# A gated mix of two long convolutions on one core: earlier stores of finished columns, two buffers of P rows, work moved to VectorE, a new order

## The chip, the core and the metric

The kernel runs on one core of a Trainium2 chip. The metric is device time in microseconds (us), the median of several runs. Engines are called as in the profile: PE (TensorE, matrix products; its weight loads are PEld), DVE (VectorE), ACT (ScalarE), POOL (GpSimd) and SP (SyncE, which here only issues DMAs). SP, ACT and POOL each issue DMAs from a queue of their own; all DMAs run on the same 16 DMA engines.

## What is computed

The input x is [2048, 448] (time, channel). A gate weighs two branches:

```python
g = sigmoid((x * gate_w).sum(-1, keepdims=True))
# branch A, per channel d: 256 complex modes
dt = exp(log_dt);  P = exp(dt * A * l)          # l = 0..2047
K  = einsum("dn,dnl,dn->dl", C, P, dt * B).real
a  = causal_conv(x, K) + x * Dskip              # by FFT of length 4096
# branch B
kv = shift_conv4(k) * v
b  = x * (causal_conv(kv, ssm_k) + kv * ssm_D)
out = g * a + (1 - g) * b
```

All arrays are bfloat16; the convolutions are 2048 long and causal, one per channel and branch.

## The kernel before

The convolutions are done by transforms written as matrix products, for 28 channels of each of four groups at a time, that is for 112 columns of work. H = 0 to 3 counts these column groups (`NQG = 4`, `NC = 28`). A convolution of branch B or A for one H goes through `spread_in` (products ps_c, copied by ACT into a tile zs), `transform` (ps_2 or ps, copied back to zs), a product with the transformed kernel on DVE (`products`), `stage_a` (ps_a, copied into a tile U) and `stage_b` (ps_b), whose result goes to an epilogue. The product also needs a copy of one operand with its two partition halves exchanged, zsS; `swapped` makes it with two DMAs on SP. zs, zsS, zsK and U share one pool of `NBQ = 7` buffers (tag q); a new tile waits until the last reader of the buffer is done.

The kernel K of branch A is made in eight blocks j (two for each H, class `KGen`). `Tables.levels` and `reals` fill a table ET of powers: phases on DVE (ks_ph), then sine and exponential on ACT, then a product on DVE. Of each pair cos, sin a negated copy of the first is kept as a third row (lines 652 to 661): for the Q levels by `nc.scalar.mul` on ACT, for the P levels on DVE. From ET, DVE doubles up two sets of rows: TQ, 32 rows for both blocks of an H (`q_rows`), and TP, 32 rows for each block (`block`, line 458). TP's rows 0 to 7 come from three doublings (`mult`, then `add`). Rows 8 to 15 are a sum of two products: one goes into a tile kg_P4 (kg_P in the profile), one into TP itself, and a DMA from POOL with `accum_op=ALU.add` adds the first to the second (lines 478 to 483). Rows 16 to 31 are the mirrored rows 0 to 15 times a real factor (`back`). `back(8, 16)` reads rows 0 to 7, `back(0, 8)` reads rows 8 to 15 and so waits for that DMA. 224 small products of TQ and TP follow into pk, whose copy kg_S goes through `gather` (ps_g, kg_KT) and `spread` (ps_c) into the tile zsK. The tile kg_TP has a single buffer: the rows of a block may be written only when the products of the block before have read theirs.

The last convolution, A of H = 3, is cut into halves (`transform_half`, `stage_a_half`, `last`), with block 7 between. `mix` weighs the two branches for each H on DVE in the tile ug, which is vt: for H below 3 a weighing of each and a sum, for H = 3 only the part of branch B, as branch A arrives last. Then `stage_b` with one bank runs `epilogue_A(3)` four times, each time for 16 of the 64 time steps that a partition holds: a product with the gate (ept), a sum into vt, and `store`, four DMAs of 32 partitions x 16 x 112 columns, two on SP and two on ACT.

At the start, ssm_D is added to a column of the loaded ssm_k by POOL (`sk_cols`). Constants lie in a tile scratch, which has the buffer that TP takes over later.

No engine's order comes from the program text. All calls are recorded (`Order`) and issued in the order of the string `ORDER`, which lists them by number; each engine works its own part strictly in that order. All recorded instructions therefore carry one line in the profile, L148, and are told apart by their tiles. DMAs of SP and ACT take one of eight completion semaphores each; a DMA whose semaphore was used by an earlier one waits for that one first.

## Time and profile before

| | us |
|---|---|
| three runs | 277.46, 279.8, 280.59 (median 279.8) |
| the profiled execution | 277.69 |
| its span, first to last instruction | 275.8 |
| DVE, ACT, PE busy | 241.7, 226.7, 210.7 |
| last product of block 7 into pk, end | 246.2 |
| last matmul, end | 264.1 |
| last DVE instruction, end | 266.2 |

A matmul's row gives its time in the pipeline, so PE's sums of durations are larger than its busy time. DVE and ACT instructions that follow each other overlap a little in the record. A row such as `L148 DVE TENSOR_TENSOR kg_TP<-kg_P 128x896 bf16<-128x896 bf16 x8 | 5.0, 625 | 0.1` says: eight such instructions, 5.0 us busy together, 625 ns each on average, and 0.1 us in which DVE stood idle before them. In lists of waits the three numbers are the time in all, how often, and the longest. The engine SPq in such a list is SP's queue of DMAs.

### The profile page before, as it was taken

How to read it: one execution, taken by the hardware profiler on the slowest of the kernel's cores; microseconds unless marked ns; L12 is line 12 of the kernel's file. 1: busy time of each engine (PE TensorE's matmuls, PEld its weight loads, DVE VectorE, ACT ScalarE, POOL GpSimd, SP SyncE). 2: the span in 40 equal slices, each digit the busy share in tenths (PEclk: the TensorE clock that was granted, in tenths of full speed). 3: DMA queues.
4: the chain of work that ended last, by engine and by line, in shares of the span. 5: the costliest groups of instructions: out<-in, count | busy, mean ns of one | idle time of the engine just before them, and what ended most of it. 6: DMA issues, size and time to landing. Idle time of an engine off the chain costs nothing.

```text
span 275.8 us, 12739 instructions
## 1 busy us (share of the span) xinstructions
PE 210.7 (76%) x5770; PEld 193.3 (70%) x5770; DVE 241.7 (88%) x488; ACT 226.7 (82%) x383; POOL 15.9 (6%) x51
## 2 busy tenths in 40 slices
PE   0610958879988799798997789867887999699830
PEld 0500858877887798687995779766886899688820
DVE  7599899999989799979996899899999997967950
ACT  2795696999899999998998799999999989546400
POOL 8000000000400000100010001001001001000000
PEclk9999999999999899998998999999999999979975
DMA  7999799607804500390093019003042263600077
GB/s 149 224 204 172 131 235 175 99 1 153 118 5 91 116 5 4 83 186 5 5 209 47 5 50 199 10 2 70 6 90 64 54 138 60 147 5 2 2 141 127
DMA packets 55110, 24.74 MB, mean 90 GB/s; under 512 B 49680, under 2 KB 52368, under 8 KB 55056
## 3 DMA queue, kind: packets, MB, share of 16 engines
q1 hardware_dynamic: 48640, 19.34, 37.7%
q0 software_dynamic: 1152, 3.67, 7.2%
q10 hardware_dynamic: 5264, 0.92, 2.1%
q8 instruction: 45, 0.74, 1.2%
q14 instruction: 9, 0.07, 0.1%
HBM read 7.95 MB, written 2.87 MB: 39 GB/s over the span
## 4 chain that ended last, share of the span: by engine, by line
ACT 38%; PE 29%; DVE 15%; DMA 9%; issue 5%; SPq 0%; DVEq 0%; POOL 0%; POOLq 0%; ACTq 0%
ACT zs L148 15%; ACT ET L148 7%; ACT U L148 6%; DMA kg_TP<-kg_P 6%; PE pk L148 5%; PE ps_a L148 5%; PE ps L148 5%; PE ps_c L148 5%; PE ps_b L148 5%; ACT zsK L148 5%; DVE vt L148 2%; DVE scratch L148 2%; PE ps_g L148 2%; PE ps_gate L148 2%; DMA skraw<-in_B_ssm_k_dram 2%
## 5 line engine op out<-in xcount | busy, mean ns | idle before, releaser
L148 ACT CAST zs<-ps 128x896 bf16<-128x896 f32 x48 | 44.0, 944 | 1.0 <-PE ps L148 0.6
L148 ACT CAST zs<-ps_c 128x1024 bf16<-128x1024 f32 (+1 forms) x48 | 42.7, 937 | 1.3 <-PE ps_c L148 1.2
L148 PEld LDWEIGHTS <-front 128*32 128x32 bf16 (+1 forms) x496 | 19.1, 159 | 27.3 <-issue 22.3
L148 PEld LDWEIGHTS <-s_W 128*128 128x128 bf16 x544 | 28.9, 100 | 12.7 <-issue 9.6
L148 PE MATMUL pk<-kg_TP,kg_TQ 128*32 128x32 bf16 x1792 | 33.2, 242 | 5.1 <-issue 2.9
L148 PEld LDWEIGHTS <-kg_TQ 128*32 128x32 bf16 x1792 | 31.2, 160 | 7.0 <-issue 4.8
L148 PE MATMUL ps_a<-sa_R,zs 128*128 128x128 bf16 x224 | 32.7, 235 | 0.3
L148 ACT CAST U<-ps_a 128x1024 bf16<-128x1024 f32 (+1 forms) x30 | 27.2, 936 | 6.9 <-PE ps_a L148 6.7
L148 PE MATMUL ps_b<-U,sb_G 128*128 128x28 bf16 x1024 | 29.5, 175 | 4.1 <-issue 1.4
L148 PE MATMUL ps_a<-sa_R,zsS 128*128 128x128 bf16 x224 | 32.1, 232 | 0.5 <-DVE zsS L148 0.5
L148 PE MATMUL ps<-zs,s_W 128*128 128x112 bf16 x384 | 27.7, 220 | 5.5 <-ACT zs L148 4.2
L148 PEld LDWEIGHTS <-sb_G 128*128 128x128 bf16 x1024 | 27.8, 96 | 5.8 <-issue 3.2
L148 DVE TENSOR_TENSOR kg_TP<-kg_TP,ET 128x1792 bf16<-128x1792 bf16 x24 | 26.1, 1090 | 5.8 <-DMA kg_TP<-kg_P 5.0
L148 PEld LDWEIGHTS <-zsS 128*128 128x128 bf16 x224 | 29.6, 152 | 1.3 <-DVE zsS L148 0.7
L148 PEld LDWEIGHTS <-zs 128*128 128x128 bf16 x224 | 29.4, 151 | 0.8
L148 PE MATMUL ps_v<-front 128*32 128x336 bf16 (+3 forms) x448 | 16.0, 310 | 16.0 <-DVE front L148 13.1
L148 ACT ACTIVATE ET<-ks_ph 128x448 bf16<-128x448 int16 x40 | 23.2, 602 | 4.1 <-DVE kg_P L148 2.6
L148 DVE TENSOR_TENSOR kg_TQ<-kg_TQ,ET 128x896 bf16<-128x896 bf16 (+1 forms) x36 | 24.8, 730 | 0.0
L148 DVE TENSOR_TENSOR kg_P<-kg_TP,ET 128x1792 bf16<-128x1792 bf16 (+1 forms) x24 | 22.4, 934 | 0.1
L148 PE MATMUL ps_c<-Wc,uu 128*64 128x128 bf16 x224 | 18.4, 290 | 1.6 <-ACT U L148 0.6
L148 PE MATMUL ps_c<-Wc,vt 128*64 128x128 bf16 x224 | 17.1, 285 | 1.4 <-ACT zs L148 1.2
L148 PEld LDWEIGHTS <-uu 128*64 128x64 bf16 x224 | 16.5, 210 | 2.4 <-issue 1.5
(102 smaller groups left out, 427.4 us busy)
## 6 DMA issues: line engine op xcount, KB each, us to landing
zsS<-zs SPq DMA_DIRECT2D x16, 448.0 KB, 5.7
kg_TP<-kg_P POOLq DMA_DIRECT2D x8, 448.0 KB, 5.7
vt<-in_B_v_dram SPq DMA_DIRECT2D x4, 448.0 KB, 6.8
skraw<-in_B_ssm_k_dram SPq DMA_DIRECT2D x16, 112.0 KB, 4.8
uu<-in_A_u_dram SPq DMA_DIRECT2D x4, 448.0 KB, 8.5
ks_xf<-xfd SPq DMA_DIRECT2D x3, 336.0 KB, 3.3
out_dram<-vt ACTq DMA_DIRECT2D x8, 112.0 KB, 3.8
out_dram<-vt SPq DMA_DIRECT2D x8, 112.0 KB, 3.6
```

What stands on the lines that cost most here:

```text
L148: ins = f(*args, **kw)
```

## The change

Six edits, and a new order for all calls:

- `mix` stores columns 0 to 83 of each group (H below 3) with four DMAs on SP, after the sums; `store` then writes only columns 84 to 111 in each of its 16 DMAs. A row of the first kind has 168 bytes, one of the second 56, where it had 224.
- TP lies in one tile of 48 rows, taken once. Rows 0 to 15 of it serve even blocks, 16 to 31 odd ones, 32 to 47 hold the mirrored rows of every block. The matmul's access pattern steps from the first kind to the second by `far`. `NBQ` goes from 7 to 6; scratch, which has the same buffer, grows with it.
- In block 7, rows 8 to 15 are made by two `mult` and two `add` on DVE; in the others the sum by DMA stays, in a function `summed`.
- The negations of the Q levels run on DVE.
- The addition of ssm_D runs on DVE.
- `ORDER` is replaced as a whole.

```diff
-NBQ = 7
+NBQ = 6
...
+    def summed(self, dst, src, r, m):
+        n = src.shape[1]
+        part = self.pool.tile([P, 8 * 2 * M], bf16, name="kg_P4", tag="kg_P4", bufs=2)[:, 0:n * 2 * m]
+        for c, out in enumerate((part.rearrange("p (n v m) -> p n v m", n=n, v=2), dst)):
+            self.nc.vector.tensor_tensor(out=out, in0=src[:, :, c].unsqueeze(2).to_broadcast([P, n, 2, m]),
+                                         in1=bass.AP(r.tensor, r.offset + c * m, [list(r.ap[0]), [0, n], [-m, 2], [1, m]]), op=ALU.mult)
+        self.nc.gpsimd.dma_start(dst.rearrange("p n v m -> p (n v m)"), part, accum_op=ALU.add)
...
-        TP = self.pool.tile([P, 32, 2, M], bf16, name="kg_TP")
+        if j == 0:
+            self.TA = self.pool.tile([P, 48, 2, M], bf16, name="kg_TP")
+        TP, late = self.TA[:, 16 * (j % 2):16 * (j % 2) + 16], self.TA[:, 32:48]
+        far = 16 * (2 - j % 2)
...
-            V.tensor_tensor(out=TP[:, 16 + i0:16 + i1], in0=src,
+            V.tensor_tensor(out=late[:, i0:i1], in0=src,
...
-        part = self.pool.tile([P, 8, 2 * M], bf16, name="kg_P4", tag="kg_P4", bufs=2)
-        r = EP[:, entry_of(64) - EQ_N + 1]
-        for c, out in enumerate((part.rearrange("p n (v m) -> p n v m", v=2), TP[:, 8:16])):
-            V.tensor_tensor(out=out, in0=TP[:, 0:8, c].unsqueeze(2).to_broadcast([P, 8, 2, M]),
-                            in1=bass.AP(r.tensor, r.offset + c * M, [list(r.ap[0]), [0, 8], [-M, 2], [1, M]]), op=ALU.mult)
-        nc.gpsimd.dma_start(TP[:, 8:16].rearrange("p n c m -> p (n c m)"), part.rearrange("p n x -> p (n x)"), accum_op=ALU.add)
+        if j == NBLK - 1:
+            add(8, mult(TP[:, 0:4], 64))
+            add(12, mult(TP[:, 4:8], 64))
+        else:
+            self.summed(TP[:, 8:16], TP[:, 0:8], EP[:, entry_of(64) - EQ_N + 1], M)
...
-                        rhs = bass.AP(r0.tensor, r0.offset, [list(r0.ap[0]), [32 * M + (1 - 2 * c) * M, 2], [2 * M, 16]])
+                        rhs = bass.AP(r0.tensor, r0.offset, [list(r0.ap[0]), [2 * M * far + (1 - 2 * c) * M, 2], [2 * M, 16]])
...
-                    nc.scalar.mul(B[:, :, 2], B[:, :, 0], -1.0)
+                    V.tensor_scalar(out=B[:, :, 2], in0=B[:, :, 0], scalar1=-1.0, scalar2=None, op0=ALU.mult)
...
-        nc.gpsimd.tensor_tensor(out=raw[:, :, 0], in0=raw[:, :, 0], in1=dB[:, H * NC:(H + 1) * NC], op=ALU.add)
+        V.tensor_tensor(out=raw[:, :, 0], in0=raw[:, :, 0], in1=dB[:, H * NC:(H + 1) * NC], op=ALU.add)
...
-    cons = Consts(nc, wp, kgp.tile([P, 3584], i32, name="scratch", tag="kg_TP"))
+    cons = Consts(nc, wp, kgp.tile([P, 5376], i32, name="scratch", tag="kg_TP"))
...
-    def store(b0, n):
+    def store(b0, n, c0, c1):
         for g in range(4):
-            dmae[g % 2].dma_start(out4[g][:, b0:b0 + n, :], ug[g * 32:(g + 1) * 32, b0:b0 + n, :])
+            dmae[g % 2].dma_start(out4[g][:, b0:b0 + n, c0:c1], ug[g * 32:(g + 1) * 32, b0:b0 + n, c0:c1])
...
-            store(b0, n)
+            store(b0, n, (NQG - 1) * NC, 112)
...
+        done = (NQG - 1) * NC
+        for g in range(4):
+            nc.sync.dma_start(out4[g][:, :, 0:done], ug[g * 32:(g + 1) * 32, :, 0:done])
```

## The prediction

> **What bounds the kernel now.** I read the whole span first: the page's engine table, then four stretches of it, cut at the first ScalarE copy of a transform (48 us), at the end of the seventh block's pk product (225), at the last matmul (264.2) and at the last packets (274).

> ```profile
> PE 210.7 (76%) x5770; PEld 193.3 (70%) x5770; DVE 241.7 (88%) x488; ACT 226.7 (82%) x383; POOL 15.9 (6%) x51
> ```
> ```profile
> 0.00:48.00 48.00, 22.13 (x520) 19.94 (x521) 42.16 (x141) 33.32 (x63) 6.67 (x41) 1.00 1.08 184
> 48.00:225.00 177.00, 153.46 (x4208) 140.44 (x4207) 166.09 (x305) 169.35 (x289) 8.33 (x9) 0.97 0.36 70
> 225.00:264.20 39.20, 35.14 (x1053) 32.93 (x1046) 31.63 (x40) 24.01 (x33) 0.85 (x1) 0.96 0.20 42
> 264.20:274.00 9.80, 0.00 (x0) 0.00 (x0) 1.86 (x4) 0.00 (x0) 0.00 (x0) 0.54 1.03 181
> ```
> Columns after the length: PE, weight loads, DVE, ACT, POOL, clock, DMA share, GB/s. So there are four limits. At the start DVE has 5.8 us free of 48 and ACT 14.7. In the middle ACT has 7.7 free of 177 and DVE 10.9: both carry it. From 225 to the last matmul PE has 4.1 free of 39.2. After that it is DMA alone: share 1.03, 181 GB/s, PE and ACT done; DVE ends at 266.2, the packets at about 273.5.

> Next, what DVE waited for in all, and its order of time around the last block.

> ```profile
> DVE kg_TP L148 <- DMA kg_TP<-kg_P: 5.0, 3, 2.1
> ...
> DVE kg_KT L148 <- PE ps_g L148: 3.4, 1, 3.4
> ...
> DVE kg_TP L148 <- PE pk L148: 1.4, 2, 0.8
> ```
> ```profile
> 225.20 0.28 DVE L148 TENSOR_TENSOR kg_TP<-kg_P 128x224 bf16<-128x224 bf16 x1 [0.56 <-PE pk L148]
> ...
> 230.52 1.08 DVE L148 TENSOR_TENSOR kg_TP<-kg_TP,ET 128x1792 bf16<-128x1792 bf16 x1
> ...
> 235.69 1.09 DVE L148 TENSOR_TENSOR kg_TP<-kg_TP,ET 128x1792 bf16<-128x1792 bf16 x1
> ```
> The P rows of block 7 start only when the product of block 6 has read theirs (225.2); their last step starts at 235.69, after the accumulating DMA, so 11.6 us pass from free buffer to finished rows.

> The rows that price the edits, by shape (busy, mean ns, idle before), and three waits of SP:

> ```profile
> L148 ACT ACT_TABLE_LOAD x11 | 14.1, 1283 | 2.9 <-issue 2.8
> ...
> L148 ACT ACTIVATE ET<-ET 128x448 bf16<-128x448 bf16 x8 | 5.1, 638 | 1.0 <-DVE ET L148 1.0
> ...
> L148 DVE TENSOR_TENSOR kg_TP<-kg_P 128x896 bf16<-128x896 bf16 x8 | 5.0, 625 | 0.1
> ...
> L148 DVE TENSOR_SCALAR ET<-ET 128x448 bf16<-128x448 bf16 x8 | 2.2, 274 | 0.0
> ...
> L148 ACT ACTIVATE ET<-ET 128x224 bf16<-128x224 bf16 x4 | 1.8, 440 | 0.0
> ```
> ```profile
> SPq L148 <- PE ps_a L148: 20.5, 4, 8.0
> ...
> SPq L148 <- DMA out_dram<-vt: 2.7, 3, 1.9
> SPq L1040 <- DMA out_dram<-vt: 2.5, 2, 2.1
> ```

> The execution profiled took 277.69 us, its span 275.8, so 1.9 lie outside. The three runs are 277.46, 279.8 and 280.59: the median is 2.1 above the profiled one. I sum against 277.7 and add 2.1 at the end.

> **Q negations.** Twelve leave ACT: 8 x 638 + 4 x 440 = 6.9 us, three of them in the start, so 6 x 638 + 3 x 440 = 5.1 in the middle. DVE takes them at its own negation row, 274 ns, less the 0.09 by which DVE instructions overlap in order of time (229.52 + 1.08 ends after the next start, 230.52): 12 x 0.19 = 2.2, of which 1.7 in the middle.

> **D added on DVE.** Four additions of 128x28 leave POOL. No DVE row has that shape; the nearest are 145 ns (one column) and 268 ns (128x224): 0.6 to 1.1 us in all, I take 0.7, nearer the small shape. On POOL they stood only before the accumulating DMAs; nobody else waited there.

> **P rows in two buffers.** The first 16 rows alternate, the mirrored 16 stay single and still wait for the product before. In DVE's new order the work between the second multiplication and the step that needs the DMA is 7 to 22 us in six blocks (before: 5 to 10); the DMA lands 4.3 to 8.2 us after its issue, 0.85 more on POOL. One block (6) keeps 4.7. So of the 5.0 us that DVE waited for this DMA I take 4 off, between 2 and 5, and the 1.4 for pk goes. The cover is DVE's own work; if that comes late, up to 1.5 us a block return.

> **Last block summed on DVE.** Two multiplications stay two multiplications; two additions of 896 come in: 2 x (0.625 - 0.09) = 1.1 us on DVE, and POOL's 0.85 plus the landing go. Only the two mirrored steps and the additions stand behind the product of block 6: 1.0 + 1.1 + 1.0 = 3.1 us where 11.6 passed.

> **Middle, 48 to 225.** ACT loses 5.1 of work. DVE gains 1.7 + 0.4 and loses 4 + 0.6 of waiting: 2.5 less. Were each free of the other, the stretch would be 2.5 to 5 us shorter; waits between engines move rather than vanish, so I take 2.0, with bounds +2.1 (only the added DVE work shows) and -5.1. The rest of the new order moves work and adds none. On SP up to four loads of skraw now stand ahead of the first swap, 4 x 0.62 = 2.5 us of issue; that swap went out at 63.0 and lands 5.7 later, and DVE's product first reads it at 79.6, so 11 us hide it.

> **End, 225 to the last DVE step.** The 8.5 us that the P chain loses can give no more than PE's 4.1 us of slack, since nearly all its 35.1 us remain behind block 6. Late next is PE itself; DVE's share (31.6 + 1.1 + mixing) is just below. I take -3.0, bounds 0 and -4.1.

> **Start.** The built order has 16 table loads for 11, and all five extra ones stand before ACT's first copy of a transform: 5 x 1.283 = 6.4 us, less three negations (1.7): 4.7 more on ACT. It had 14.7 us free there, while DVE, the bound, has 0.7 more work before the last product into vt. I take 0, bounds -1 and +4.7.
> [...]

> **Stores.** Before, 16 DMAs of 512 packets of 224 bytes: 8,192 packets keep the 16 DMA engines busy from 263 to 273.5. Now the 16 move 56 bytes a packet, and four more of 2,048 packets of 168 bytes go out first, on SP. The trace's packet records give 13.0 ns for 8 bytes (mean), 15.7 for 128, 19.0 for 224 on ACT's queue. Between them I put 56 bytes at 14.1 and 168 at 17.1: 8,192 x 14.1 / 16 = 7.2 us and 8.8 us, against 10.5 us of DMA share summed over the tail before. The early four are released by the third addition of the mixing; 9.8 us of DVE work stand behind it in the new order. They need about 3 us to issue and land near DVE's end; DMAs were idle there (share 0.02 from 240 to 260). SP's third and fourth late stores take their completion semaphores over from early ones, and so wait for them, with the rest of SP's queue behind. So the late stores end between 0.4 + 3.2 = 3.6 us after DVE's end (last issue and shortest landing) and 7.3 (as before). I take 5.3: -2.0.

> Sum: -2.0 - 3.0 + 0 - 2.0 = -7.0; 277.7 - 7.0 = 270.7; with 2.1, 272.8. I say 273.

> **Rivals.**
> A packet costs the same at 56 bytes as at 224. For it: 8-byte packets take 13.0 ns, not a twenty-eighth of 19.0. Against: 128 bytes have 15.7. Then the late stores again need 10.5 us and the tail is as long as before: 275. [...] Chance 0.10.
> The waits only move: DVE keeps the 24.5 us in which it stood until 266.2 (266.2 - 241.7), and its 2.2 + 0.7 + 1.1 = 4.0 us come on top, with the tail's -2.0: 281.8. For it: three engines carry the middle. Against: the waits for the accumulating DMA are named. Chance 0.13.
> The start: all 4.7 us of added ACT work show, since ACT ends the start (its first copy waits at 48): 277.5. Against: 14.7 us free. Chance 0.09.
> Slower: six large working buffers for seven. Before, SP's swap DMAs already waited 20.5 us in four waits for a stage A (ps_a) to give a buffer free. With one buffer less each swap after the first may go out one stage later: 56 matmuls, 63 ns from start to start, 3.5 us; seven convolutions, 24.5 us. Against: no compute engine is named as waiting for a swap, so it has slack, 40.7 us of SP's waits being for DVE instead. It outweighs the gain of 7 once 0.29 of it shows; at a half it is 273 + 12.3 = 285. Chance 0.18.

> **Chances.** The forecast has 0.50, nearly all below 277.0 (1% under 279.8, about what a measurement can tell from no change); with the first rival and a third of the start that makes 0.60 faster. Within 1%: most of the second rival, the rest of the third, 0.18. Slower by over 1%: the buffers and the worst of the moved waits, 0.22. The forecast's own range is 266 (-5.1, -4.1, -3.7 and -1 together: 263.8 + 2.1) to 277. For eight in ten I go to 283: that takes in the moved waits and the start, and leaves out the larger part of the buffers.

> **What would show it.** The middle: DVE no longer waits for kg_TP's DMA, and the seventh pk ends before 223. The end: from that to block 7's pk under 8 us, not 12. The start: ten table loads, the first transform copy still at 47 to 49. The tail: packets end 4 to 6 us after DVE's last step. Wrong if ACT or PE stand waiting for zs or U buffers, if swaps go out late, or if early and late stores overlap in full.

## The result and the profile after

The changed kernel took 296.25 us (median of 4 runs, 295.42 to 297.6), the kernel before 278.63 beside it (276.57 to 280.59): a ratio of 1.064, 95% interval 1.054 to 1.074. Forecast were 273, with 266 to 283. Here and below a median is over all executions, while ratios and intervals go by the undisturbed ones alone, so a ratio is not quite the quotient of two medians. The profiled execution after has a span of 294.8 us, 19.0 more than before.

The page's table of engines, after:

```profile
PE 215.0 (73%) x5770; PEld 195.6 (66%) x5770; DVE 244.3 (83%) x506; ACT 230.0 (78%) x376; POOL 11.6 (4%) x46
```

DVE has 2.6 us more to do, ACT 3.3, PE 4.3: nothing that makes 19. So I cut the span at the same four events as in the prediction: the first ScalarE copy of a transform, the end of the seventh block's pk product, the last matmul, the end. The stretches of after (columns as in the prediction):

```profile
0.00:51.50 51.50, 23.33 (x528) 20.94 (x528) 42.43 (x145) 39.45 (x66) 5.41 (x39) 0.93 1.01 176
51.50:232.20 180.70, 158.80 (x4233) 144.43 (x4234) 170.07 (x322) 167.77 (x280) 6.20 (x7) 0.92 0.32 64
232.20:270.90 38.70, 32.87 (x1012) 30.25 (x1010) 30.03 (x38) 22.78 (x31) 0.00 (x0) 0.96 0.44 71
270.90:294.80 23.90, 0.00 (x0) 0.00 (x0) 1.80 (x4) 0.00 (x0) 0.00 (x0) 0.57 1.04 40
```

Against the stretches of before (48.0, 177.0, 39.2 and, up to the span's end at 275.8, 11.6) that is +3.5, +3.7, -0.5 and +12.3. The last stretch is DMA alone at 40 GB/s, where before had 181. The middle's +3.7 can be placed by one more event, the first product into pk. The row of the pk products, with the first and the last start, in before and then in after:

```profile
L148 PE MATMUL pk<-kg_TP,kg_TQ x1792: 214/241/267, 77.8 to 245.9; 128*32 128x32 bf16 x200
```
```profile
L148 PE MATMUL pk<-kg_TP,kg_TQ x1792: 215/241/268, 85.0 to 245.3; 128*32 128x32 bf16 x200
```

It starts 7.2 us later. From there to the end of the seventh block's product the two kernels take 147.3 and 147.2 us (77.8 to 225.1, 85.0 to 232.2). So the account is: start +7.2, middle 0, end -0.5, stores +12.3. The last block itself begins 4.2 us after the seventh (236.4) where it was 11.9, and ends at 245.5, no later than before; but 27.3 us pass from there to DVE's last step where 20.1 did, because the new order has left more of the last convolutions and of the mixing behind it: 593 matmuls instead of 461.

The waits of after's whole span that answer to those of before, and two of SP's queue:

```profile
DVE kg_KT L148 <- PE ps_g L148: 7.0, 1, 7.0
...
DVE kg_TP L148 <- PE pk L148: 4.9, 3, 2.5
...
PE pk L148 <- DMA kg_TP<-kg_P: 2.4, 1, 2.4
...
DVE kg_P L148 <- DMA kg_TP<-kg_P: 1.4, 2, 0.9
...
DVE kg_TP L148 <- DMA kg_TP<-kg_P: 0.5, 2, 0.3
```
```profile
SPq L148 <- PE ps_a L148: 31.4, 4, 11.3
...
SPq L148 <- DMA out_dram<-vt: 9.1, 5, 3.5
```

DVE's wait for the accumulating DMA is down from 5.0 to 1.9 (the last two rows). In its place stand 4.9 for pk (was 1.4) and 7.0 for ps_g (was 3.4): together they are 13.8 where 9.8 stood, and PE has 2.4 of its own for the DMA. In SP's queue the waits for ps_a are up from 20.5, and stores wait 9.1 us for the semaphores of earlier stores, 2.7 before.

### The profile page after: what moved, and what is told of

It reads as the page before. It is cut to its first block, busy times and chain, and to the rows that moved or that the text cites. A ratio compares the mean times of both kernels' runs of the same rounds, so it can differ in the third digit from the quotient of the medians.

```text
span 294.8 us, 12748 instructions
## 1 busy us (share of the span) xinstructions
PE 215.0 (73%) x5770; PEld 195.6 (66%) x5770; DVE 244.3 (83%) x506; ACT 230.0 (78%) x376; POOL 11.6 (4%) x46
## 3 DMA queue, kind: packets, MB, share of 16 engines
q10 hardware_dynamic: 5264, 0.24, 3.4%
## 5 line engine op out<-in xcount | busy, mean ns | idle before, releaser
L148 ACT CAST zs<-ps 128x896 bf16<-128x896 f32 x48 | 42.8, 936 | 5.4 <-PE ps L148 5.3
L148 ACT CAST zs<-ps_c 128x1024 bf16<-128x1024 f32 (+1 forms) x48 | 42.9, 941 | 0.4 <-PE ps_c L148 0.2
L148 PE MATMUL pk<-kg_TP,kg_TQ 128*32 128x32 bf16 x1792 | 35.7, 241 | 6.6 <-DMA kg_TP<-kg_P 2.4
L148 PEld LDWEIGHTS <-front 128*32 128x32 bf16 (+1 forms) x496 | 19.9, 160 | 29.6 <-issue 24.4
L148 PEld LDWEIGHTS <-kg_TQ 128*32 128x32 bf16 x1792 | 32.3, 159 | 9.2 <-issue 5.7
L148 PEld LDWEIGHTS <-s_W 128*128 128x128 bf16 x544 | 30.4, 104 | 10.3 <-issue 8.2
L148 PE MATMUL ps_a<-sa_R,zs 128*128 128x128 bf16 x224 | 32.6, 233 | 1.5 <-DVE zs L148 1.0
L148 ACT CAST U<-ps_a 128x1024 bf16<-128x1024 f32 (+1 forms) x30 | 27.1, 931 | 6.9 <-PE ps_a L148 4.8
L148 PE MATMUL ps_b<-U,sb_G 128*128 128x28 bf16 x1024 | 30.1, 176 | 3.1 <-issue 1.7
L148 PEld LDWEIGHTS <-sb_G 128*128 128x128 bf16 x1024 | 28.1, 97 | 5.9 <-issue 3.2
L148 PE MATMUL ps<-zs,s_W 128*128 128x112 bf16 x384 | 28.5, 225 | 4.5 <-ACT zs L148 4.3
L148 PE MATMUL ps_a<-sa_R,zsS 128*128 128x128 bf16 x224 | 31.7, 230 | 0.0
L148 PEld LDWEIGHTS <-zs 128*128 128x128 bf16 x224 | 29.3, 150 | 2.3 <-DVE zs L148 1.4
L148 PEld LDWEIGHTS <-zsS 128*128 128x128 bf16 x224 | 29.6, 152 | 0.6 <-issue 0.5
L148 PE MATMUL ps_v<-front 128*32 128x336 bf16 (+3 forms) x448 | 17.0, 318 | 15.8 <-DVE front L148 8.2
L148 DVE TENSOR_TENSOR kg_TP<-kg_TP,ET 128x1792 bf16<-128x1792 bf16 x23 | 24.9, 1084 | 3.0 <-PE pk L148 2.5
L148 ACT ACTIVATE ET<-ks_ph 128x448 bf16<-128x448 int16 x40 | 22.6, 584 | 5.3 <-DVE ks_ph L148 5.2
L148 DVE TENSOR_TENSOR kg_TQ<-kg_TQ,ET 128x896 bf16<-128x896 bf16 (+1 forms) x36 | 25.0, 718 | 0.0
L148 DVE TENSOR_TENSOR kg_P<-kg_TP,ET 128x1792 bf16<-128x1792 bf16 (+1 forms) x25 | 23.3, 935 | 0.2
L148 ACT ACT_TABLE_LOAD x16 | 20.5, 1283 | 2.0 <-issue 1.8
L148 DVE TENSOR_TENSOR kg_P<-kg_TQ,ET 128x1792 bf16<-128x1792 bf16 (+1 forms) x20 | 17.8, 895 | 1.4 <-DMA kg_TP<-kg_P 1.4
L148 PE MATMUL ps_c<-Wc,uu 128*64 128x128 bf16 x224 | 18.2, 299 | 0.8 <-ACT zs L148 0.7
## 6 DMA issues: line engine op xcount, KB each, us to landing
out_dram<-vt SPq DMA_DIRECT2D x4, 336.0 KB, 11.2
```

The costliest lines, as they stand in the source:

```text
L148: ins = f(*args, **kw)
```

## The experiments

In each run only what the diff shows is changed, and in ORDER the places of calls that are added, left out or moved; the diffs are put in short. "before" and "after" name the kernel it starts from. Ratios are to the kernel before, run beside it. The tail of a trace is the time from DVE's last step to the end of the span.

### The stores

`s1_before_split`: before, with the change's stores alone.

```diff
-            store(b0, n)
+            store(b0, n, (NQG - 1) * NC, 112)
...
+    done = (NQG - 1) * NC
+    for g in range(4):
+        nc.sync.dma_start(out4[g][:, :, 0:done], ug[g * 32:(g + 1) * 32, :, 0:done])   # after the third sum of mix
```

> The kernel before with one part of the change: columns 0 to 83 stored by four DMAs on SP as soon as the third column group is mixed, the last stores cut to columns 84 to 111. The order is that of before, in which the third group is mixed just ahead of the last convolution's first output. Theory S (the cut stores are dearer, packet by packet, and are the larger part of the loss): last DVE step near 266 as before, then 20 to 24 us of packets instead of 9.6, so 289 to 294 us. Theory O (the new order is what costs, the stores are harmless): 276 to 281 us.

296.19 us, 1.064 (1.056 to 1.073): as much as the whole change loses, from this part alone, and more than Theory S had. DVE's last step stands at 264.6, the span ends at 292.4: a tail of 27.8 us, before 9.6. In the order of before the third sum ends late (260.1), so early and late pieces go out together here.

`s2_after_whole`: after, with the stores of before.

```diff
-            store(b0, n, (NQG - 1) * NC, 112)
+            store(b0, n, 0, 112)
...
-            nc.sync.dma_start(out4[g][:, :, 0:done], ug[g * 32:(g + 1) * 32, :, 0:done])
```

> The changed kernel with the stores as before: whole rows of 112 columns after each piece of the last convolution, no early DMAs. Theory S: last DVE step near 273, packets end some 10 us later, 282 to 285 us. Theory O: the time stays at 294 to 298 us.

287.3 us, 1.030 (1.021 to 1.040): some 9 us come back; 3.0% of loss stay. That is between the two theories: the stores are about half of the loss in the order of after, and the rest lies elsewhere.

`s3_after_late_only`: after, only the four early DMAs taken out.

> The changed kernel without the four early DMAs: columns 0 to 83 are left out of the output, only the 56-byte pieces are stored. It tells whether a 56-byte packet is slow in itself. If the time of a packet hangs on its own size or place alone, 4096 packets on each queue at some 30 ns over 16 engines keep the tail at 15 to 20 us: 288 to 293 us. If they are slow only because they run against the early DMAs' packets, the tail is 8 to 10 us: 281 to 284 us.

289.27 us, 1.039 (1.031 to 1.046). A quarter of the bytes, in as many packets, takes no less time than whole rows did (2.0 us more than s2, with intervals that overlap): the 56-byte pieces are dear without any early ones beside them. But 7.0 of the 9 us come only with the early four. In the trace of after their packets run from 262.9 to 281.1, 8.2 us past DVE's last step, and SP's late packets begin at 278.3. What is dear about these pieces, the next run tells.

`s4_after_cut80`: after, the cut moved by four columns.

```diff
-        done = (NQG - 1) * NC
+        done = 80
...
-            store(b0, n, (NQG - 1) * NC, 112)
+            store(b0, n, 80, 112)
```

> The changed kernel with the cut at column 80 in place of 84: 160-byte and 64-byte packets, each at a multiple of 32 bytes in the output's row, the same number of packets as in the changed kernel. If the place of a piece against 32 bytes sets its time: tail 10 to 14 us, 283 to 288 us. If the number of packets and two pieces in one stretch of memory set it: 293 to 298 us as in the changed kernel.

285.41 us, 1.024 (1.017 to 1.031): 10.8 us less than after, with the same number of packets and the same bytes in all. The early packets now end at 272.7, with DVE's last step at 273.0, and the tail is 8.6 us. The queues and the landing of the output's DMAs in before, after and s4_after_cut80, from the pages (queue: packets, MB, share of 16 engines; DMA: count, KB each, median us to landing):

```profile
q10 hardware_dynamic: 5264, 0.92, 2.1%
...
out_dram<-vt ACTq DMA_DIRECT2D x8, 112.0 KB, 3.8
```
```profile
q10 hardware_dynamic: 5264, 0.24, 3.4%
...
out_dram<-vt SPq DMA_DIRECT2D x4, 336.0 KB, 11.2
...
out_dram<-vt ACTq DMA_DIRECT2D x8, 28.0 KB, 8.9
```
```profile
q10 hardware_dynamic: 5264, 0.27, 1.3%
...
out_dram<-vt SPq DMA_DIRECT2D x4, 320.0 KB, 7.1
...
out_dram<-vt ACTq DMA_DIRECT2D x8, 32.0 KB, 3.9
```

ACT's queue has the same 5,264 packets each time. With a quarter of the bytes its time rises from 2.1% to 3.4% of the span; with four columns more a piece it is 1.3%. The packet records of the traces show how:

```
kernel              bytes  queue  packets  mean ns  median   95%   99%  above 100 ns
before                224    ACT     4096     19.0      16    33    39     0
after                  56    ACT     4096     36.0      11   207   488   351
after                 168     SP     8192     34.8      15   120   385   482
s3_after_late_only     56    ACT     4096     33.4      11   178   445   351
s4_after_cut80         64    ACT     4096     11.2      11    20    42     2
s4_after_cut80        160     SP     8192     15.2      13    25    32     0
o4_before_cut48       128    ACT     4096     13.5      13    21    27     1
p2_before_cut56       112    ACT     4096     24.9      13    86   260   176
```

The usual packet has become cheaper with its size, as forecast (median 11 ns for 56 bytes, 16 for 224). But 4 to 9% of the packets of a cut that is no multiple of 32 bytes take more than 100 ns, and they set the mean: in after's row of 56 bytes the 351 have 66% of the packets' time, and the mean of the rest is 13.4 ns. In the rows on the 32-byte grid, where every piece begins and ends on a multiple of 32 bytes of the output's row, it is at most 2 packets of 4,096. A multiple of 16 alone, the 112 bytes of p2 below, has 176 of them. A multiple of 64 is not needed here: a group's row of 224 bytes, as before stores it, begins 32 bytes past one in every second group, and none of its 4,096 packets takes that long. Nor does it take two stores that meet in the same 32 bytes: in s3, with 351 of 4,096, nothing else writes the 32 bytes that a piece begins in.

`o4_before_cut48` and `p2_before_cut56`: before, with early stores once the second group is mixed (near 246), cut at column 48 (96 and 128 bytes) or at 56 (112 and 112 bytes, one end of each piece off the grid).

```diff
-            store(b0, n)
+            store(b0, n, 48, 112)      # p2: 56
...
+    for g in range(4):
+        nc.sync.dma_start(out4[g][:, :, 0:48], ug[g * 32:(g + 1) * 32, :, 0:48])   # p2: 56
```

> The kernel before with its stores cut at column 48: columns 0 to 47 (96-byte packets) go out on SP once the second group is mixed, near 246 us, when the DMA engines are idle, and the last stores carry columns 48 to 111 (128-byte packets); every piece lies at a multiple of 32 bytes. Theory S in its refined form (whole 32-byte units are fast, and a packet's time then goes with its size): 13 to 15 ns a packet instead of 20, so the tail falls from 9.6 to 6 or 7 us: 275 to 277 us. If a cut store always loses: 282 us or more. If the tail is set by something other than packets: 278 to 280 us.

> Run o4_before_cut48 (0.986 of before) with the cut at column 56 in place of 48: early and late pieces are both 112 bytes, of which half begin and all end off the 32-byte grid or the other way round; the number of packets and the time of the early stores are the same. If the place against 32 bytes sets the time: the last stores take 8 to 12 us longer than in o4, 283 to 290 us. If the number of packets and their size set it: 275 to 278 us as in o4.

o4: 276.77 us, 0.986 (0.977 to 0.995), faster than before, though its four executions spread from 273.8 to 279.4. p2: 288.16 us, 1.038 (1.032 to 1.043). The tails are 7.5 us (o4) and 13.6 (p2), before 9.6. So the last stores take 6.1 us longer off the grid, not the 8 to 12 of the theory, although the time lies in its range: the other 5.6 us between the two traces arose ahead of DVE's last step, 3.5 of them ahead of the last pk product, where the two programs are the same and p2's trace ran longer at half clock (see the last section).

### The start

`o1_before_start_after`: before, its first 923 calls in the order of after. `o5_before_start_after_act`: the same, but ACT's own calls there in the order of before.

```diff
-    "0-1 540 2 945 947 23 886 559 533 553-554 896-897 560 31 13 544 538 542-543 967 36 946 539 546 549 60 12 551 22 "
...
+    "962 1 553 2 955-956 953 561 954 957 540 964 559 562 554 947 916 948 15 538 8 60-61 3 889 0 12 565 22 31 11 16 "
...
```

> The kernel before, all its edits as before, but with the first 923 calls (those up to the eighth copy of a zs tile, the table building of the start) issued in the order of the changed kernel; the rest follows in the order of before. The changed order brings ten table loads ahead of the first zs copy instead of five. Theory T (the start's delay is carried to the end, since nothing later has room to take it up): first pk matmul near 84 instead of 77.8, 284 to 287 us. Theory R (the delay is taken up by idle time in the middle): 278 to 281 us.

> Run o1_before_start_after (289.3 us: the kernel before with the start issued in the order of the changed kernel), but ScalarE's own calls of the start stay in the order of before, so that five table loads lie ahead of the first zs copy instead of ten. If the five extra loads (6.4 us) are what delays the start: 279 to 284 us. If the order on the other engines delays it: 286 to 290 us.

o1: 289.32 us, 1.034 (1.028 to 1.040); first copy at 53.3, first pk product at 86.7 (before 77.8), DVE's last step at 277.8 (266.2). The delay is carried to the end and grows by 2.7. o5: 286.74 us, 1.031 (1.026 to 1.036); first copy at 49.7, first pk product at 83.1. So ACT's part of the order, with its five extra table loads, costs the smaller part of o1's 10.6 us (2.6 by the medians, 0.3% by the ratios, whose intervals overlap; 3.6 at the first pk product), and the order on the other engines the larger. Of after's ten loads, five stand between 36.08 and 50.4 (ACT in order of time: start, duration, operation):

```profile
36.08 1.28 ACT L148 ACT_TABLE_LOAD   x1
...
38.62 1.28 ACT L148 ACT_TABLE_LOAD   x1
39.91 2.02 ACT L148 ACTIVATE sb_ph<-sb_ph 128x1024 bf16<-128x1024 int16 x2
...
45.21 1.28 ACT L148 ACT_TABLE_LOAD   x1
...
47.20 1.28 ACT L148 ACT_TABLE_LOAD   x1
...
49.09 1.28 ACT L148 ACT_TABLE_LOAD   x1
```

`o2_cut80_start_before`: s4_after_cut80 with its first 907 calls in the order of before, as far as six buffers allow. `n1_cut80_seventh_room`: the same, and one of the four phase tables of the start moved into the part of the scratch tile that nothing uses; the order of the start, which the seventh room allows to follow that of before further, differs from o2's at 83 of 6,763 places.

```diff
-            both = qt([P, 1536], "sb_ph", i32)
+            both = self.scratch[:, 3584:5120] if b0 == 16 else qt([P, 1536], "sb_ph", i32)   # n1 alone
```

> The changed kernel with its stores cut at column 80 (run s4_after_cut80: 285.4 us) and the start issued in the order of before (its first 907 calls, as far as six buffers allow; five table loads). Theory T: first pk matmul near 78, 278 to 280 us. Theory R: 284 to 287 us as without it. If six buffers themselves hold the start up, the first pk matmul stays near 85 although the table loads are five.

> Run o2_cut80_start_before (301.7 us: the changed kernel, stores cut at column 80, the start issued in the order of before under six buffers) with one thing more: the second of the four phase tables of the start lies in the unused third of the P rows' tile instead of in one of the six buffers, so that the start has room for seven. Theory N (the missing seventh buffer holds the start up): first zs copy back near 48 to 50 from 54.8, first pk matmul near 78 to 82 from 94.8, 280 to 288 us. Rival (the two orders do not fit at the seam, whatever the room): 296 to 302 us.

o2: 301.65 us, 1.082 (1.072 to 1.091), the first copy comes at 54.8 and the first pk product at 94.8: all three theories missed it. This stitched order, made for seven buffers, is slower under six than the changed one. n1: 296.41 us, 1.058 (1.050 to 1.067), first pk product at 89.5: by the ratios the seventh room and the order fitted to it give some 6 us back, far less than its theory wanted, and the median lies in its rival's range. That six buffers hold the start up in part is likely from this; how much of it they are in the changed kernel is not shown, since an order stitched from two has losses of its own at the seam.

### The middle

`o3_before_qneg`: before, Q negations on VectorE. `e2_before_no_qneg`: left out of the later chunks. `e3_before_less_dve`: three products on DVE left out. `n3_before_both_less`: both left out.

```diff
-                    nc.scalar.mul(B[:, :, 2], B[:, :, 0], -1.0)
+                    V.tensor_scalar(out=B[:, :, 2], in0=B[:, :, 0], scalar1=-1.0, scalar2=None, op0=ALU.mult)   # o3
...
+                    if not h: nc.scalar.mul(B[:, :, 2], B[:, :, 0], -1.0)                                       # e2, n3
...
-    for t in (S, X):
+    for t in (S, X) if both else (X,):                                                                          # e3, n3
```

> The kernel before with one part of the change: the Q negations on VectorE, order unchanged. By the prediction's bookkeeping ScalarE, which limits the middle, gets 5.1 us less work there and VectorE 1.7 us more: 274 to 277 us. If the instructions' fixed order turns the saved time into waits: 278 to 280 us. If VectorE, as busy as ScalarE, is the limit: 280 to 282 us.

> The kernel before without the Q negations of the three later table chunks (that part of the computation is left out): ScalarE has some 5 us less to do in the middle, VectorE the same as before. If ScalarE limits the middle, as the prediction had it: 273 to 276 us. If VectorE limits it: 278 to 280 us. Together with run o3 it tells what ScalarE's relief is worth without VectorE's burden.

> The kernel before without three of the middle's products on VectorE (the swapped halves of B1, A0 and B2 stay unmultiplied: that part of the computation is left out): 3 x 2.02 = 6.1 us less on VectorE, ScalarE the same as before. If VectorE limits the middle: 272 to 275 us. If ScalarE limits it: 278 to 280 us. If each is late in turn: in between, 275 to 278 us.

> The kernel before without the Q negations of the later chunks and without three of the middle's products (the parts of the computation that e2 and e3 left out one at a time): some 5 us less on ScalarE and 6 us less on VectorE. If the two engines limit the middle in turn, so that relief of one alone shows nothing: 272 to 275 us. If waits in the fixed order limit it: 277 to 279 us.

o3: 280.39 us, 1.006 (1.003 to 1.009). e2: 278.03, 0.999 (0.995 to 1.002). e3: 277.77, 0.998 (0.995 to 1.002). n3: 277.01, 0.999 (0.995 to 1.002). o3 lies between its second and third theory; e2 and n3 lie in their ranges for no gain, and e3 0.2 us below its own. Five to six microseconds off ACT, off DVE or off both give no gain clear of the noise; the intervals leave room for 0.5%, 1.4 us. The stretch from the first pk product to the end of the last, before and then n3:

```profile
77.80:246.20 168.40, 146.56 (x4310) 135.05 (x4309) 154.47 (x275) 155.65 (x269) 6.35 (x8) 0.96 0.32 68
```
```profile
78.00:245.90 167.90, 147.56 (x4309) 136.09 (x4309) 148.57 (x272) 152.94 (x260) 6.36 (x8) 0.94 0.32 68
```

DVE's busy time fell by 5.9 us, ACT's by 2.7 (by 6.8 if its rows, which overlap, are added up), the stretch by 0.5: the freed time has become waits, at a mean clock of 0.94 where before has 0.96.

`p1_before_half_pk`: before, half of the pk products of blocks 1 to 6 left out.

```diff
+                        if hf and 0 < j < NBLK - 1:
+                            continue
```

> The kernel before without the second half of the pk products in blocks 1 to 6 (896 - 224 = 672 of the 1792 matmuls left out: that part of the computation is missing): by the undisturbed block of 224 matmuls in 3.9 us, 6 x 1.95 = 11.7 us less on TensorE, the other engines the same as before. If TensorE's work and the chains that run through it bound the middle: 268 to 272 us. If the middle is bound by none of the three engines' work: 277 to 280 us.

285.62 us, 1.023 (1.015 to 1.031): with 672 matmuls fewer the kernel is slower, which no theory had. The page's engine table and its row of the granted clock (40 slices, tenths of full speed), for p1 and below it the clock of before and of after:

```profile
PE 212.6 (75%) x5098; PEld 193.5 (68%) x5098; DVE 241.9 (85%) x488; ACT 228.0 (80%) x383; POOL 19.8 (7%) x51
...
PEclk9999979999999757996886699757779899869955
```
```profile
PEclk9999999999999899998998999999999999979975
```
```profile
PEclk9999869979999799986797999899799979999655
```

PE has 672 matmuls less and is busy 1.9 us longer than before: between 80 and 246 us the granted clock is 0.83 where before has 0.96.

`n5_cut80_qneg_act`: s4_after_cut80 with the Q negations back on ScalarE.

> Run s4_after_cut80 (285.4 us) with the Q negations back on ScalarE, order unchanged. If their place on VectorE delays the start as it did in run o3 (first pk matmul 2.2 us later): 282 to 284 us. If the changed order has made room for them on VectorE: 286 to 290 us.

297.01 us, 1.070 (1.064 to 1.075): 11.6 more than s4, more than either theory had. Waits between 203 and 240 us:

```profile
DVE kg_P L148 <- ACT ET L148: 8.1, 1, 8.1
PEld L148 <- DVE kg_TQ L148: 7.4, 1, 7.4
```

At the place that the order gives them, the negations stand behind ScalarE's copies; DVE waits 8.1 us for one and PE behind it 7.4. The same edit costs 0.6% in the order of before and saves 4% in that of after.

### The last block, and the parts that helped

`e1_before_lastsum`: before, block 7's rows 8 to 15 summed on DVE. `n2_before_cut48_lastsum`: this and the stores of o4.

```diff
+        if j == NBLK - 1:
+            add(8, mult(TP[:, 0:4], 64))
+            add(12, mult(TP[:, 4:8], 64))
+        else:
...
```

> The kernel before with one part of the change: the last block's P rows 8 to 15 summed on VectorE (two products and two sums, in place of two products and the summing DMA), all else and the order as before. By the prediction's end term (-3.0, bounds 0 and -4.1): 275 to 277 us. If the chain's end is set by something else once the DMA is gone: 278 to 280 us.

> The kernel before with the two parts that helped alone: the stores cut at column 48 (run o4: 0.986 of before) and the last block's P rows summed on VectorE (run e1: 0.992). If they add up: 0.978 of before, 272 to 273 us. If the one hides the other: 275 to 277 us.

e1: 276.19 us, 0.992 (0.988 to 0.995), 2.2 us less, as its first theory had. But its trace does not show the way to it that this theory took. DVE in order of time, in before and then in e1, up to the last step of block 7's P rows:

```profile
233.55 2.02 DVE L148 TENSOR_TENSOR zsS<-zsS,zsK 128x3584 bf16<-128x3584 bf16 x1 [1.95 <-ACT zsK L148]
235.69 1.09 DVE L148 TENSOR_TENSOR kg_TP<-kg_TP,ET 128x1792 bf16<-128x1792 bf16 x1
```
```profile
237.77 1.08 DVE L148 TENSOR_TENSOR kg_TP<-kg_TP,ET 128x1792 bf16<-128x1792 bf16 x1
```

In before the DMA's last packet ends at 235.2, while DVE is still at the product into zsS, for which it had waited 1.95 us, and not for the DMA. Without the DMA the rows are ready 11.4 us after their buffer is free (227.5 to 238.9), with it 11.6. Block 7's pk products begin 11.9 us after the seventh block's in both, because PE has other matmuls between them in its order. From the seventh product's end to the last matmul e1 and n2 take 37.1 us, and the ten traces of before's order that have the DMA 37.2 to 40.2 (before 38.9). So the gain is shown by ten executions, and it likely lies in this stretch; by what way it comes stays open.

n2: 274.92 us, 0.990 (0.985 to 0.995). The two don't add up to 0.978; n2's median is the lowest measured, and its interval overlaps with those of e1 and o4 alone.

## Why the prediction was wrong

**Stores, forecast -2.0 (bounds 0 and -3.7): +12.3 in the profiled executions, 9.0 by s2_after_whole.** This step failed at the price of a packet: 56 bytes were put at 14.1 ns and 168 at 17.1 by interpolation over size, and took 36.0 and 34.8 on average. Of the three rows behind it only that of 224 bytes was a store into the output; the packets of 8 and 128 bytes were loads (shift_k and ssm_k). What the price went with in these runs is whether a piece begins and ends on a multiple of 32 bytes of the output: in the table above the pieces of 56, 112 and 168 bytes, which do not, took 24.9 to 36.0 ns, and those of 64, 128, 160 and 224, which do, 11.2 to 19.0. The early four were to land near DVE's end and ran on 8.2 us past it, with SP's late stores behind them; by s3 that is 7.0 of the 9.0 us. On the grid size does count as forecast, and is cheaper still: 64 bytes take 11.2 ns, 160 take 15.2. The step was sound once that is met: s4 against s2 is 285.41 against 287.3, -1.9 where -2.0 stood (their intervals overlap; the tails are 8.6 and 10.2). The traces show the slow packets, not what the memory does with them. The first rival was too mild: 56 bytes are not as dear as 224 but dearer (36.0 ns against 19.0 on ACT's queue).

**Start, forecast 0 (bounds -1 and +4.7): +7.2 at the first pk product.** The step that failed counted ACT's added work against ACT's idle time, as if any idle time could take it. By o1 the new start order alone costs 10.6 us in the kernel before; by o5 ACT's part of it, with the loads, is the smaller. The rival with the start's 4.7 us named the right mechanism for that smaller part. The larger lies in the order on the other engines, which the forecast put at nothing; six buffers may share in it (n1 against o2), and so may the clock (last section).

**Middle, forecast -2.0 (bounds +2.1 and -5.1): 0 from the first pk product to the seventh's end.** The step that failed is the reading that ACT's and DVE's small idle shares (7.7 and 10.9 us of 177) make them the limits. e2, e3 and n3 took that work off and got nothing clear of the noise. Likely, but shown by no run, is that with each engine held to a fixed order the path changes over from one to another many times: the chain that ended last in before has 38% of the span on ACT, 29% on PE, 15% on DVE and 9% on DMA. Then the time of a stretch isn't the work of its busiest engine. The rival in which waits only move fits this stretch. The waits for the accumulating DMA did go in the main (5.0 to 1.9 on DVE, with 2.4 new ones on PE), and came back as waits for pk and ps_g. The 0 itself is not exact: six traces with before's program in this stretch (before, s1, o4, p2, e1, n2) take 146.0 to 149.4 us, with 10.2 to 27.3 us of it at half clock. After has 23.9 us at half clock where before has 10.2, so a gain of a microsecond or two may be hidden in it.

**End, forecast -3.0 (bounds 0 and -4.1): -0.5 in the change; alone, in e1, -0.8%, 2.2 us.** The step that failed is the reading that block 7's last P step at 235.69 waits for the DMA. It stood behind a product that waited for ACT, and with the DMA gone the rows took 11.4 us where 11.6 passed, not 3.1 (in one buffer; the second one was not run alone). e1's time lies in the forecast, but not by the mechanism that was named. The 4.2 us from the seventh product to the eighth came with the new order, as e1 keeps 11.9. That order also left 132 more matmuls for after the last block, which took back nearly all of it.

**The rival on six buffers** put their price on late swaps. SP's waits for ps_a did grow, from 20.5 to 31.4 us, but the middle lost nothing by it; if the buffers counted, it was at the start, where four phase tables compete for them.

Of what was to show it, the ten table loads and the short gap to block 7 came true, the gap for another reason. The seventh product's end (232.2 for 223), the first copy (51.5 for 47 to 49) and the end of the output's packets (19.3 us after DVE's last step for 4 to 6) did not. One sign of being wrong came true: early and late stores overlapped.

## What to carry over

Cut a store like this one only where every piece begins and ends on a multiple of 32 bytes of the output: on that grid at most 2 of 4,096 packets took more than 100 ns, off it 4 to 9%. Four columns decided 10.8 us here, and a cut on the grid in the old kernel gained 1.4% (0.5 to 2.3). Before the time between two events is put down to one wait, look at what the engine did in between, and whether it stood idle for that cause at all. In a kernel whose engines follow a fixed order, count no gain from work taken off a busy engine until one run with that work left out has shown it, and put no price on an edit apart from the order in which it stands. A delay ahead of a stretch in which all engines are nine tenths busy was paid in full at the end here (o1).

## What the runs showed of the hardware

```
clock in window   PE busy share   windows   next at half clock
full              below 0.60           68                   63
full              0.60 to 0.75        171                   61
full              above 0.75          881                    9
half              below 0.80           37                   34
half              0.80 to 0.90         26                   12
half              above 0.90          116                    0
```

So of the windows at full clock 93% below a busy share of 0.60 were followed by half clock, 36% from there to 0.75, and 1% above. Of those at half clock 3 of 37 were followed by full clock below 0.80, 14 of 26 from there to 0.90, and all 116 above: the way back went with more work than the fall. Of the 133 falls, 118 had no gap of 3.41 us between matmuls in the window ahead, 103 none of 2 us (median of the longest gap: 1.19). Most falls thus came without an idle stretch of that length; what besides the busy share has a part in a fall is not shown.

Up to the last matmul the clock was at half for 13.7 us in before, 37.5 in after, 69.2 in p1, 64.9 in o2, 17.1 in o4 and 34.1 in p2. The transforms' products (ps<-zs, 112 columns) start 93 ns apart at half clock, otherwise 49 (medians in before and after); the pk products, with 32 columns, show no difference (16 ns on average in both). Nine other traces with the start of before have their first pk product at 77.8 to 78.0 where no such spell lay ahead of it (s1, o4, p2, n3), and at 78.5 to 79.6 where one did (e1, e2, e3, n2, p1), before itself at 77.8 with none. In after three windows of 3.41 us at half clock, 10.2 us, lie ahead of it: at 0.7 to 1.8 us each they would make 2 to 5 of its +7.2, an estimate from those nine.

That the clock is why p1 is slower, and why work taken off elsewhere gains nothing, is likely from these numbers (p1's own executions, with spans of 284.1, 284.6, 283.3 and 280.3 us, had mean clocks of 0.856, 0.867, 0.875 and 0.900), but no run here holds the clock and changes the work alone.
